# A planned kernel of attention, experts and a gated MLP: later planned landings, attention's tiles dealt out anew, a new order

## The chip, the cores and the metric

The kernel runs on one core of a Trainium2 chip. The metric is the device time of one execution in microseconds, the median of several runs. A profile is one further execution, taken by the hardware profiler. The engines of the core are TensorE (PE in the rows), VectorE (DVE), ScalarE (ACT), GpSimd (POOL) and SyncE (SP), which only issues transfers here. Each has a list of instructions of its own, which it works through in order.

## The reference

Three layers follow each other. The first is causal attention with a memory read beside it, over 4 batches, 8 heads, 576 positions and 64 columns:

```
scores = scale * q @ k.T ; causal ; a = softmax(scores) ; local = a @ v
q_p = where(q > 0, q, exp(q) - 1) + 1
mem_out = (q_p @ M_prev) / (q_p @ z_prev + 1e-6)
x = g * mem_out + (1 - g) * local          # g = sigmoid(beta)
```

The second sends each of the 2304 rows of x (512 wide) to one of 8 experts:

```
logits = x @ w_gate + modality_bias[modality_id] ; e_idx = argmax(logits)
out[rows of e] = gate_w * (relu(x @ w1[e]) @ w2[e])      # 512 -> 1024 -> 512
```

The third is a gated MLP over all rows, with weights of 512 x 1536, 512 x 1536 and 1536 x 512:

```
(silu(x @ w_gate) * (x @ w_val)) @ w_out
```

Everything is float32. The kernel gets that precision from fast products: an operand is split into a high and a low part, and three products (high x high, high x low, low x high) take the place of one.

## The kernel before, in words

The work runs in three phases that touch at their ends. **Attention** takes the 16 pairs of heads (4 in each batch) one after another, up to about 257 us of the profiled execution. For a pair, `pair(n)` turns k and q by TensorE into operands (L345, L351, and L362, L363 for the last 64 positions; they use the accumulator bank `prep`), splits them into high and low parts in a tile `HL`, makes the scores (L402 and L417, banks `ps`), masks them and takes the row maximum on VectorE (L410, L420, from `ps` into a tile `SS`), exponentiates on ScalarE (L422, `SS` into `PF`), turns the probabilities by TensorE (L432 into the banks `tp`, L441 into `mm`), copies them (L437, L438, into `pt`) and multiplies by v (L456 into the bank `LN`; L445 for the last 64 positions, into the bank `mm`). The memory products L377 read `mb` and `qp` and go into `mm` as well, and VectorE reads them in L380 to L384, and the result of L445 in L477. After each batch `route` computes the gate (L491, L497), using the modality ids `mi`, which VectorE casts once in L550. Near the end of attention, one expert is begun early: TensorE counts (L556), a register is read on SP, `rows()` reads three lists of 100 row numbers into `it` (L646), TensorE turns them (L647), GpSimd gathers the rows by them into `xr` (L652), and TensorE turns these (L654).

**The experts** follow, up to about 499 us: for blocks of 300 rows, `rows()` as before, then h products (L682 to L684) and y products (L670 to L672), with weights loaded in pieces of 512 KB into `raw` and split by `split`. **The gated MLP** is the rest: the products L787 to L789 (gate and value, into banks `gv`) and L805 to L807 (output, banks `po`). Its weights are converted by `split64` from 512 KB pieces of raw words: ScalarE L631, VectorE L633 to L636, ScalarE L637 (the high part) and GpSimd L638 (the low part). The last weights, in a place called `wC`, are still being converted while the products of this phase run.

The order is made by a planner, `Sched.run`, when the kernel is built. Each instruction or small group is a task with an engine, a duration as assumed, tasks that it needs, tiles that it takes from a pool and gives back, and a priority; in attention the table `PRM['off']` adds to the priority of each kind of task. The planner takes, over and over, the engine that can start first, and on it the task of best priority among those within the slack. For a transfer it assumes a landing:

```
s.way=max(s.way,t['end']+w)+t['dd']; t['lat']=s.way+w+200-t['end']+t['late']
```

So `late` is a time by which a transfer is assumed to land later. It is no wait on the chip; it sets where the planner puts the tasks that need the data. The order that results on each engine is fixed, and on the chip an instruction waits by semaphores for what it needs.

Of the kernel before, what the change touches and what calls it, by code (L numbers as in the profile page):

```python
# [10 lines left out]
F32 = mybir.dt.float32  # L11
F32R = mybir.dt.float32r
# [6 lines left out]
PSUM = bass.MemoryType.PSUM  # L19
# [8 lines left out]
def ac(n): return 60+.83*n  # L28
def po(n): return 150+2.1*n


PRM={'US': 1807, 'slack': 69, 'ps': (3, 2, 1, 1, 1), 'dcopy': (0,), 'off':{
# [10 lines left out]
NW=24; NC=4  # L43
# [8 lines left out]
class Sched:  # L52
# [18 lines left out]
    def add(s,eng,dur,fn,deps=(),acq=(),use=(),prio=0.0,lat=None,name='',ph=None):  # L71
# [5 lines left out]
        s.todo.append(t); return t  # L77
    def dma(s,fn,deps=(),acq=(),use=(),prio=0.0,nbytes=0,eng='SP',name='',ph=None,few=False,late=0.):
        t=s.add(eng,(650 if few else 500) if eng=='SP' else 1265,fn,deps,acq,use,prio,lat=1500+nbytes/360.,name=name,ph=ph)
        t['late']=late; t['dd']=max(30.,nbytes/360.); return t  # L80
    def ready(s,t):
# [95 lines left out]
class Net:  # L177
# [303 lines left out]
    warm=PRM.get("warm",(8,2,3))  # L481
# [132 lines left out]
    def split(s,src,prio,ph,lo_eng,deps=(),name=''):  # L614
        nc=s.nc; sc=s.sc; raw,hi,lo=sc.tok('raw'),sc.tok('w'),sc.tok('w')
        def f(): x=src(); nc.sync.dma_start(out=raw.tile.rearrange("p (k f) -> p k f",k=x.shape[1]),in_=x)
        d=sc.dma(f,deps=deps,acq=[raw],prio=prio,nbytes=524288,name='dw'+name,ph=ph,late=4000. if ph==2 else 2000. if ph==1 else 0.)
        a=sc.add('ACT',ac(1024)+37,lambda: nc.scalar.activation(out=hi.tile,in_=raw.tile,func=AF.Copy),deps=[d],acq=[hi],use=[raw],prio=prio,name='wh'+name,ph=ph)
        e=nc.gpsimd if lo_eng=='POOL' else nc.vector
        b=sc.add(lo_eng,po(1024) if lo_eng=='POOL' else dv(1024),lambda: e.tensor_tensor(lo.tile,raw.tile,hi.tile.bitcast(F32),op=ALU.subtract),deps=[a],acq=[lo],use=[raw,hi],prio=prio,name='wl'+name,ph=ph)  # L620
        return hi,lo,[a,b]

    def split64(s,src,prio,ph,name=''):
        nc=s.nc; sc=s.sc; hi,lo=sc.tok('w'),sc.tok('w'); dd=[]
        for h in range(2):
            raw,c=sc.tok('raw'),sc.tok('c'); sl=slice(512*h,512*h+512); p=prio+h
            def f(h=h,raw=raw): x=src(h); nc.sync.dma_start(out=raw.tile.bitcast(I32).rearrange("p (k f) -> p k f",k=x.shape[1]),in_=x)
            d=sc.dma(f,acq=[raw],prio=p,nbytes=524288,name='dw'+name,ph=ph,late=3000.)
            Hw=lambda raw=raw: raw.tile.bitcast(I32).rearrange("p (n w) -> p n w",w=2)[:,:,1]
# [14 lines left out]
    def rows(s,row,deps,prio,ph,ps,name='',nb=None):  # L644
        nc=s.nc; sc=s.sc; n=s.W//3; it,ii,xh,xl=sc.tok('it'),sc.tok('ii'),sc.tok('xh'),sc.tok('xl'); tp0=sc.tok(ps)
        d=sc.dma(lambda: s.after('ids',nc.sync.dma_start(out=it.tile,in_=s.idsE[bass.ds(row(),s.W),:].rearrange("(a c) o -> a (c o)",a=3))),deps=deps[0],acq=[it],prio=prio,name='id'+name,ph=ph,late=1000.)  # L646
        a=sc.add('PE',10,lambda: nc.tensor.transpose(tp0.tile[0:n,0:3],it.tile,s.ident[0:3,0:3]),deps=[d],acq=[tp0],use=[it],prio=prio+.1,name='it'+name,ph=ph)  # L647
        a=sc.add('DVE',75,lambda: nc.vector.tensor_copy(ii.tile[0:n],tp0.tile[0:n,0:3]),deps=[a],acq=[ii],use=[tp0],prio=prio+.2,name='ic'+name,ph=ph)
        dd=[]
        for j in range(3):  # L650
            xr=sc.tok('xr'); tp=sc.tok(ps); cs=slice(n*j,n*j+n)
            g=sc.dma(lambda j=j,xr=xr: nc.gpsimd.indirect_dma_start(out=xr.tile[0:n],out_offset=None,in_=s.xg if nb is None else s.xg[0:1+nb*s.S],in_offset=bass.IndirectOffsetOnAxis(ap=ii.tile[0:n,j:j+1],axis=0)),eng='POOL',deps=[a]+deps[1],acq=[xr],use=[ii],prio=prio+.3,nbytes=204800,name='gx'+name,ph=ph,late=2000.)  # L652
            def f(tp=tp,xr=xr):
# [192 lines left out]
def kernel(ctx0: ExitStack, tc: tile.TileContext, *aps: bass.AP):  # L846
# [4 lines left out]
    with ExitStack() as c0, tc.manual_schedule():  # L851
# [13 lines left out]
        for i,(k,k2) in enumerate((('xh','yh'),('xl','yl'))):  # L865
            v=[t.rearrange("p k c -> p (k c)")[:,0:4*W].rearrange("p (k c) -> p k c",k=4) for t in xx[i::2]]
            sc.pool(k,v); sc.pool(k2,[]); sc.give[k]={id(a):[(k2,t)] for a,t in zip(v,xx[i::2])}
        def some(p):
            s.tiles(p,'xr',2,[128,512]); s.tiles(p,'xtr',2,[128,4,128])
            sc.pools['raw']=sc.pools['raw'][:2]+[[p.tile([128,1024],F32,name="raw2"),0]]  # L870
# [5 lines left out]
        with ExitStack() as c1:  # L876
            pa=P(c1,"pa"); some(pa)
            for n,k,sh,dt in (('qn0',1,[128,4,256],F32),('kn0',1,[128,4,256],F32),('vn0',1,[128,5,256],F32),('qn1',1,[128,4,256],F32),('kn1',1,[128,4,256],F32),('vn1',1,[128,5,256],F32),('k4',2,[128,128],F32),
                          ('r2',1,[128,640],F32),('qp',1,[128,640],F32),('dn',2,[128,19],F32),('sm',2,[128,10],F32),('SS',2,[128,576],F32),('PF',3,[128,576],F32),('pt0',2,[128,2,256],F32),('pt2',2,[128,4,256],F32),('pt4',2,[128,640],F32),
                          ('oT',1,[128,512],F32),('t1',1,[128,4,2,64],F32),('t2',1,[128,4,2,64],F32),('t4',1,[128,128],F32)): s.tiles(pa,n,k,sh,dt)  # L880
            sc.pools['HL']+=[[pa.tile([128,2,1216],F32R,name=f"HL{i}"),0] for i in (1,2)]
            pp=P(c1,"pp",space=PSUM)
            for k,c in zip(('ps','tp','prep','LN','mm'),PRM['ps']): s.tiles(pp,k,c,[128,512])
            s.consts(pc,pa)
            s.plan1(); s.plan2(); s.plan3()
            sc.slack=PRM['slack']; sc.run(1); sc.slack=100
# [3 lines left out]
        with ExitStack() as c2:  # L890
            p2=P(c2,"p2"); some(p2); pp=P(c2,"pp2",space=PSUM)
            s.tiles(p2,'hh',3,[128,W],F32R); s.tiles(p2,'hl',3,[128,W],F32R)
# [46 lines left out]
```

## Time and profile before

| | |
|---|---|
| runs | 961.85, 962.27, 967.39 us |
| median | 962.27 us |
| profiled execution, its own time | 970.94 us |
| its span in the trace | 969.2 us |
| mean granted TensorE clock | 0.98 of full speed |
| TensorE busy | 929.1 us, 96% of the span |
| VectorE, ScalarE, GpSimd busy | 494.4, 392.1, 178.2 us |

The span is the time from the first to the last recorded instruction; 1.7 us lie around it. The profiled execution took 8.7 us longer than the median. All times inside the kernel, below and in the prediction, come from this one execution.

### The profile page before, as it was taken

To read this page: it belongs to the slowest core of one execution; us is meant where nothing else is said; L and a number is where in the kernel's file an instruction comes from. 1 tells how busy PE (TensorE), PEld (TensorE's weight loads), DVE (VectorE), ACT (ScalarE), POOL (GpSimd) and SP (SyncE) were. 2 spreads that over 40 slices of the span, in tenths; PEclk is the share of its full clock that TensorE was granted. 3 is DMA by queue.
4 is the path that set the end of the run, shared out by engine and by line. 5 is a ranking of instruction groups with operands and counts; after the bars stand their busy time and mean duration, and the time that the engine had idled before them with its cause. 6 is when DMAs were issued, how large, how long until landed. Compare 5 with 4: busy or idle time off the path is not lost. (4 is left out here: it accounts for less than half of the span.)

```text
span 969.2 us, 16634 instructions
## 1 busy us (share of the span) xinstructions
PE 929.1 (96%) x6389; PEld 846.4 (87%) x6389; DVE 494.4 (51%) x1382; ACT 392.1 (40%) x902; POOL 178.2 (18%) x199
## 2 busy tenths in 40 slices
PE   8899999997999999989989989999999999999996
PEld 7687786875798999989989989999999999999995
DVE  7787887896741538832556763223223223223221
ACT  6687888886633335412433332112112112112111
POOL 3112103122635423411221321001001001001001
PEclk9899999998999999999999999999999999999998
DMA  7444534214346634541222421001001000000000
GB/s 150 98 92 53 100 81 93 57 17 138 112 61 174 181 112 148 159 147 51 71 74 96 141 65 66 1 1 66 1 1 66 1 1 33 1 1 33 1 1 33
DMA packets 93426, 67.28 MB, mean 69 GB/s; under 512 B 67515, under 2 KB 78925, under 8 KB 93342
## 3 DMA queue, kind: packets, MB, share of 16 engines
q1 hardware_dynamic: 88797, 56.37, 23.2%
q0 software_dynamic: 4544, 9.79, 3.2%
q8 instruction: 52, 0.85, 0.4%
q14 instruction: 33, 0.26, 0.1%
HBM read 51.65 MB, written 14.49 MB: 68 GB/s over the span
## 5 line engine op out<-in xcount | busy, mean ns | idle before, releaser
L796 DVE SCALAR_TENSOR_TENSOR X<-X,gv 128x384 f32<-128x384 f32 x72 | 39.9, 554 | 188.7 <-ACT X L795 188.7
L787 PE MATMUL gv<-xx,wB 128*128 128x384 f32 x384 | 130.9, 341 | 2.0 <-PEq L822 2.0
L788 PE MATMUL gv<-xx,wB 128*128 128x384 f32 x384 | 130.7, 340 | 0.0
L789 PE MATMUL gv<-xx,wB 128*128 128x384 f32 x384 | 130.6, 340 | 0.0
L795 ACT ACTIVATE X<-gv 128x384 f32<-128x384 f32 x72 | 35.3, 491 | 199.4 <-PE gv L789 186.2
L422 ACT ACTIVATE PF<-SS,sm 128x256 f32<-128x256 f32 (+1 forms) x144 | 87.1, 607 | 12.2 <-DVE sm L410 8.8
L606 POOL DMA_INDIRECT out_dram<-X,ii x18 | 17.5, 971 | 360.5 <-ACT X L814 357.9
L787 PEld LDWEIGHTS gv<-xx,wB 128*128 128x128 f32 x384 | 72.5, 189 | 4.3 <-issue 2.2
L788 PEld LDWEIGHTS gv<-xx,wB 128*128 128x128 f32 x384 | 72.6, 189 | 1.9
L789 PEld LDWEIGHTS gv<-xx,wB 128*128 128x128 f32 x384 | 72.7, 189 | 0.0
L797 DVE TENSOR_TENSOR X<-X,gv 128x384 f32<-128x384 f32 x72 | 39.9, 554 | 63.5 <-PE gv L789 63.2
L687 DVE SCALAR_TENSOR_TENSOR hl<-h,hh 128x300 fp32r<-128x300 f32 x64 | 29.9, 467 | 77.8 <-ACT hh L686 75.5
L410 DVE CUSTOM_DVE_ANT_0 SS<-ps,mk 128x256 f32<-128x256 f32 (+2 forms) x128 | 64.5, 517 | 5.2 <-PE prep L351 1.9
L432 PE MATMUL tp<-ident,PF 128*128 128x128 f32 x384 | 63.6, 287 | 1.3 <-ACT pt L438 1.2
L438 ACT ACTIVATE pt<-tp 128x512 f32<-128x512 f32 (+2 forms) x112 | 54.6, 501 | 21.6 <-PE tp L432 16.5
L686 ACT ACTIVATE hh<-h 128x300 fp32r<-128x300 f32 x64 | 26.7, 418 | 87.1 <-PE h L684 84.3
L682 PE MATMUL h<-xx,wB 128*128 128x300 f32 x192 | 59.1, 308 | 0.0
L684 PE MATMUL h<-xx,wB 128*128 128x300 f32 x192 | 58.3, 303 | 0.0
L683 PE MATMUL h<-xx,wB 128*128 128x300 f32 x192 | 58.1, 303 | 0.0
L807 PE MATMUL po<-wB,al 128*128 128x512 f32 x144 | 56.7, 394 | 0.0
L432 PEld LDWEIGHTS tp<-ident,PF 128*128 128x128 f32 x384 | 43.6, 144 | 11.6 <-issue 3.6
L638 POOL TENSOR_TENSOR wB<-X,wB 128x512 fp32r<-128x512 f32 x24 | 33.5, 1400 | 90.0 <-ACT wB L637 52.4
(287 smaller groups left out, 2368.5 us busy)
## 6 DMA issues: line engine op xcount, KB each, us to landing
raw<-in_moe_w_dram SPq DMA_DIRECT2D x16, 512.0 KB
raw<-in_moe_w_gate_dram SPq DMA_DIRECT2D x12, 512.0 KB
raw<-in_moe_w_val_dram SPq DMA_DIRECT2D x12, 512.0 KB
raw<-in_moe_w_out_dram SPq DMA_DIRECT2D x12, 512.0 KB
yT<-X SPq DMA_DIRECT2D x8, 600.0 KB
X<-yT SPq DMA_DIRECT2D x6, 768.0 KB
kn<-in_k_dram SPq DMA_DIRECT2D x32, 128.0 KB
qn<-in_q_dram SPq DMA_DIRECT2D x32, 128.0 KB
```

The lines of the kernel that those rows point to most:

```text
L410: def f(Sp=Sp,SS=SS,i=i,N=N,c=c,so=so): nc.vector.tensor_tensor_reduce(out=SS.tile[:,0:N],in0=Sp.tile[:,so:so+N],in1=s.mk[:,512-128*i:512- ...
L422: def f(SS=SS,PF=PF,N=N,c=c): nc.scalar.activation(out=PF.tile[:,0:N],in_=SS.tile[:,0:N],func=AF.Exp,scale=-1.0,bias=sm.tile[:,c:c+1],accu ...
L432: for j in range(m+1): nc.tensor.transpose(tp.tile[:,128*j:128*j+128],PF.tile[:,128*j:128*j+128],s.ident)
L438: else: cps.append(add('ACT',ac(W),lambda pc=pc,tv=tv: nc.scalar.activation(out=pc(),in_=tv(),func=AF.Copy),deps=[Tt],prio=pu+2*US,name=f' ...
L682: nc.tensor.matmul(o,H,xh.tile[:,k],start=(k==0),stop=False)
L683: nc.tensor.matmul(o,H,xl.tile[:,k],start=False,stop=False)
L684: nc.tensor.matmul(o,Lo,xh.tile[:,k],start=False,stop=(k==3))
L787: nc.tensor.matmul(o,H,yh.tile[:,k],start=(k==0),stop=False)
L788: nc.tensor.matmul(o,H,yl.tile[:,k],start=False,stop=False)
L789: nc.tensor.matmul(o,Lo,yh.tile[:,k],start=False,stop=(k==3))
L796: a=sc.add('DVE',dv(TN),lambda th=th,g=g: nc.vector.scalar_tensor_tensor(out=th.tile,in0=th.tile,scalar=1.0,in1=g.tile[:,0:TN],op0=ALU.add ...
L807: nc.tensor.matmul(o,lv()[:,c],H,start=False,stop=(f==NF-1))
```

## The change

It has three parts. The first: the planner assumes later landings. A transfer of attention with a positive priority gets 2500 ns where it had none; the weight pieces of the experts (`split`) get 4000 in any phase that is named, where it was 2000 or 4000; those of the MLP (`split64`) 3000 or 500, where it was 3000; the row numbers (L646) 4500 or 3500, where it was 1000; the gathers (L652) 3500, where it was 2000. The second: in attention there are four tiles `xr` (before: two), three `SS` (two), four `PF` (three) and two `HL` (three). The accumulator banks stay as they were (three `ps`, two `tp`, one each of `prep`, `LN` and `mm`). The third: all numbers of the table `PRM['off']` are new. Cut to its core:

```
-    'AV,5':-0.98, 'AV,7':4.14, 'AV,8':-6, 'S,0':5.55, 'S,2':4.03, 'S,3':3.22, 'S,8':4.36, 'T,0':-4.86, 'T,1':-3.23, 'T,2':-1.64, 'T,3':-3.04,
+    'AV,5':6, 'AV,7':-5.67, 'AV,8':-4.47, 'S,0':4.42, 'S,2':5.94, 'S,3':4.15, 'S,8':3.99, 'T,0':-5.64, 'T,1':-5.59, 'T,2':-3.75, 'T,3':-5.07,
...
-    def dma(s,fn,deps=(),acq=(),use=(),prio=0.0,nbytes=0,eng='SP',name='',ph=None,few=False,late=0.):
+    def dma(s,fn,deps=(),acq=(),use=(),prio=0.0,nbytes=0,eng='SP',name='',ph=None,few=False,late=None):
-        t['late']=late; t['dd']=max(30.,nbytes/360.); return t
+        t['late']=(2500. if ph is None and s.ph==1 and prio>0 else 0.) if late is None else late; t['dd']=max(30.,nbytes/360.); return t
...
-        d=sc.dma(f,deps=deps,acq=[raw],prio=prio,nbytes=524288,name='dw'+name,ph=ph,late=4000. if ph==2 else 2000. if ph==1 else 0.)
+        d=sc.dma(f,deps=deps,acq=[raw],prio=prio,nbytes=524288,name='dw'+name,ph=ph,late=4000. if ph else 0.)
...
-            d=sc.dma(f,acq=[raw],prio=p,nbytes=524288,name='dw'+name,ph=ph,late=3000.)
+            d=sc.dma(f,acq=[raw],prio=p,nbytes=524288,name='dw'+name,ph=ph,late=3000. if ph==2 else 500.)
...
(rows: the row numbers, late=1000. -> late=4500. if ph==1 else 3500.; the gathers, late=2000. -> late=3500.)
...
-            s.tiles(p,'xr',2,[128,512]); s.tiles(p,'xtr',2,[128,4,128])
+            s.tiles(p,'xr',n,[128,512]); s.tiles(p,'xtr',2,[128,4,128])
...
-            pa=P(c1,"pa"); some(pa)
+            pa=P(c1,"pa"); some(pa,4)
...
-('SS',2,[128,576],F32),('PF',3,[128,576],F32)
+('SS',3,[128,576],F32),('PF',4,[128,576],F32)
...
-            sc.pools['HL']+=[[pa.tile([128,2,1216],F32R,name=f"HL{i}"),0] for i in (1,2)]
+            sc.pools['HL']+=[[pa.tile([128,2,1216],F32R,name=f"HL{i}"),0] for i in (1,)]
...
-            p2=P(c2,"p2"); some(p2); pp=P(c2,"pp2",space=PSUM)
+            p2=P(c2,"p2"); some(p2,2); pp=P(c2,"pp2",space=PSUM)
```

TensorE has 5111 rows of instructions before and after. Three places show what moved on it.

On TensorE near the end of attention, where the first row numbers of the early expert are turned (L647; HL2 and HL1 are copies of the tile HL, it0 and it1 the row numbers). Before:

```order
L402 MATMUL ps1_138<-HL2_133 128x512
L402 MATMUL ps0_137<-HL2_133 128x512
L432 MATMUL tp1_141<-ident_145,PF2_121 128x128 x2
L377 MATMUL mm0_144<-mb1_152,qp0_112 128x130 x3
L647 MATMUL ps2_139<-ident_145,it0_75 100x3
L351 MATMUL prep0_142<-ident_145,qn10_106 128x128 x4
L647 MATMUL ps1_138<-ident_145,it1_76 100x3
```

After:

```order
L402 MATMUL ps2_142<-HL1_136 128x256
L402 MATMUL ps0_140<-HL1_136 128x256
L362 MATMUL prep0_145<-ident_148,k41_112 128x128
L363 MATMUL prep0_145<-ident_148,q4_1_153 128x128
L647 MATMUL ps1_141<-ident_148,it0_75 100x3
L432 MATMUL tp0_143<-ident_148,PF2_124 128x128 x4
L647 MATMUL ps1_141<-ident_148,it1_76 100x3
```

The first L647 was row 866 of TensorE's list and is row 891 now; the count at L556, on which the row numbers depend, is row 792 in both. Between the two stand twelve L402 of 256 columns, ten L432, six L417, four L456, four L351, two L377, one L362 and one L363 more than before.

On TensorE between pairs 5 and 6 (L377 is the first memory product of pair 6, into the bank mm0; the last product of pair 5, L445, goes into the same bank and stands just ahead of six L402 of 384 columns in both lists, the last two of which are the first rows here). Before:

```order
L402 MATMUL ps1_138<-HL_72 128x384
L402 MATMUL ps0_137<-HL_72 128x384
L432 MATMUL tp1_141<-ident_145,PF1_120 128x128
L432 MATMUL tp0_140<-ident_145,PF0_119 128x128 x2
L351 MATMUL prep0_142<-ident_145,qn10_106 128x128 x4
L377 MATMUL mm0_144<-mb1_152,qp0_112 128x130 x3
```

After:

```order
L402 MATMUL ps1_141<-HL_72 128x384
L402 MATMUL ps0_140<-HL_72 128x384
L377 MATMUL mm0_147<-mb1_155,qp0_114 128x130 x3
L467 MATMUL tp0_143<-ident_148,oT0_132 128x128 x4
L432 MATMUL tp1_144<-ident_148,PF0_122 128x128 x2
L351 MATMUL prep0_145<-ident_148,qn10_108 128x128 x4
```

Three L432 and four L351 stood between the last L402 and L377, and nothing does now. The distance from L445 to L377 is shorter than before at the ends of pairs 1, 5, 11 and 14.

On TensorE in the expert phase, at the transposes of gathered rows (L654, from the tiles xr0 and xr1) of the sixth block. Before:

```order
L672 MATMUL y30_3379<-hl1_3370,wB14_3345 128x300
L654 MATMUL xp1_3375<-ident_145,xr0_3358 128x100 x4
L654 MATMUL xp0_3374<-ident_145,xr1_3359 128x100 x4
L682 MATMUL h1_3373<-xx2_82,wB16_3347 128x300
L683 MATMUL h1_3373<-xx3_83,wB16_3347 128x300
L684 MATMUL h1_3373<-xx2_82,wB17_3348 128x300
```

After:

```order
L682 MATMUL h1_3376<-xx2_82,wB16_3350 128x300
L683 MATMUL h1_3376<-xx3_83,wB16_3350 128x300
L684 MATMUL h1_3376<-xx2_82,wB17_3351 128x300
L654 MATMUL xp1_3378<-ident_148,xr0_3361 128x100 x4
L654 MATMUL xp0_3377<-ident_148,xr1_3362 128x100 x4
L670 MATMUL y00_3379<-hh2_3371,wB18_3352 128x300
```

The two L654 stood right behind the y products, ahead of the h products of the next step, and stand behind twelve of them now.

Two moves lie on other engines. On SP the eight loads of `mi` are the 33rd to 40th transfer of its list, where they were the 39th to 46th, and VectorE's cast of them (L550) stands ahead of two L410 of 512 columns that it stood behind. In the MLP the conversions of the last weights stand earlier on ScalarE (L631, L637) and on VectorE (L633 to L636), by about one of the steps that L795 marks; GpSimd's and SP's lists in that phase are the same.

## Rows read from the trace of the kernel before

**Rows 1.** The page: busy time by engine, and the granted clock of TensorE in 40 slices.

```profile
PE 929.1 (96%) x6389; PEld 846.4 (87%) x6389; DVE 494.4 (51%) x1382; ACT 392.1 (40%) x902; POOL 178.2 (18%) x199
...
PEclk9899999998999999999999999999999999999998
```

**Rows 2.** Waits of TensorE by releaser: us in total, times, longest us.

```profile
PE ps L647 <- DMA it<-idsE: 3.7, 1, 3.7
...
PE gv L787 <- ACT wC L637: 1.9, 1, 1.9
```

**Rows 3.** Windows: length, busy us (x instructions) of each engine, PEclk, DMA share, GB/s.

```profile
25.00:50.00 25.00, 22.03 (x192) 17.57 (x187) 18.61 (x70) 16.93 (x47) 4.14 (x5) 0.86 0.51 104
425.00:450.00 25.00, 22.71 (x157) 22.33 (x157) 5.56 (x12) 4.88 (x11) 2.00 (x2) 0.93 0.13 41
550.00:575.00 25.00, 22.28 (x107) 20.14 (x106) 16.63 (x28) 7.57 (x14) 5.14 (x4) 0.93 0.31 90
```

**Rows 4.** Timeline of VectorE, 27 to 33 us: start, duration, instruction, [idle before, releaser].

```profile
27.53 0.69 DVE L410 CUSTOM_DVE_ANT_0 SS<-ps,mk 128x512 f32<-128x512 f32 x1
...
31.19 0.18 DVE L550 CAST mf<-mi 128x20 f32<-128x20 int32 x1 [2.97 <-DMA mi<-in_moe_modality_id_dram]
```

**Rows 5.** Timeline of SP's queue, 23 to 31 us.

```profile
23.82 0.39 SPq L256 DMA_DIRECT2D mi<-in_moe_modality_id_dram  x1
...
27.81 0.52 SPq L257 DMA_DIRECT2D mi<-in_moe_modality_id_dram  x1
```

**Rows 6.** Timeline of SP's queue, 205 to 232 us.

```profile
216.13 0.74 SPq L616 DMA_DIRECT2D raw<-in_moe_w_dram  x1
220.41 0.79 SPq L646 DMA_DIRECT2D it<-idsE  x2
```

**Rows 7.** Timeline of TensorE, three places from 204 to 229 us.

```profile
204.66 0.17 PE L556 MATMUL ps<-cum,ones 128*1 128x8 bf16 x1
...
209.14 0.94 PE L377 MATMUL mm<-mb,qp 128*128 128x130 f32 x6 [0.66 <-DVE X L477]
...
228.09 0.21 PE L647 MATMUL ps<-ident,it 3*100 3x3 f32 x1 [3.68 <-DMA it<-idsE]
```

**Rows 8.** Timeline of TensorE, 242 to 246.8 us, the last pair.

```profile
242.03 0.79 PE L402 MATMUL ps<-HL 64*128 64x384 f32 x6
242.76 0.80 PE L445 MATMUL mm<-vn,pt 128*64 128x64 f32 x20
243.49 0.55 PE L432 MATMUL tp<-ident,PF 128*128 128x128 f32 x3
243.96 1.06 PE L402 MATMUL ps<-HL 64*128 64x512 f32 x6
...
245.23 0.83 PE L377 MATMUL mm<-mb,qp 128*128 128x130 f32 x6
245.82 1.03 PE L417 MATMUL ps<-HL 128*128 128x288 f32 x6
246.70 0.33 PE L432 MATMUL tp<-ident,PF 128*128 128x128 f32 x1
```

**Rows 9.** Windows at the end of attention, columns as in rows 3.

```profile
228.09:240.00 11.91, 10.30 (x69) 8.33 (x70) 9.46 (x32) 7.14 (x18) 4.44 (x3) 0.77 0.31 89
240.00:257.70 17.70, 15.45 (x154) 12.60 (x155) 15.43 (x44) 13.34 (x32) 13.63 (x9) 0.99 0.47 137
```

**Rows 10.** Timeline of TensorE in the expert phase, two places.

```profile
427.68 0.64 PE L654 MATMUL xp<-ident,xr 100*128 100x100 f32 x4 [2.29 <-DMA xr<-xg,ii]
...
490.87 0.30 PE L682 MATMUL h<-xx,wB 128*128 128x300 f32 x1
491.01 0.30 PE L683 MATMUL h<-xx,wB 128*128 128x300 f32 x1
```

**Rows 11.** Timeline of ScalarE, 509 to 521 us, two gate steps of the MLP.

```profile
514.29 0.49 ACT L795 ACTIVATE X<-gv 128x384 f32<-128x384 f32 x1 [3.41 <-PE gv L789]
...
520.58 0.49 ACT L795 ACTIVATE X<-gv 128x384 f32<-128x384 f32 x1
```

More of the change, by code (lines that the diff above doesn't have):

```diff
@@ L645, in rows @@
         nc=s.nc; sc=s.sc; n=s.W//3; it,ii,xh,xl=sc.tok('it'),sc.tok('ii'),sc.tok('xh'),sc.tok('xl'); tp0=sc.tok(ps)
-        d=sc.dma(lambda: s.after('ids',nc.sync.dma_start(out=it.tile,in_=s.idsE[bass.ds(row(),s.W),:].rearrange("(a c) o -> a (c o)",a=3))),deps=deps[0],acq=[it],prio=prio,name='id'+name,ph=ph,late=1000.)
+        d=sc.dma(lambda: s.after('ids',nc.sync.dma_start(out=it.tile,in_=s.idsE[bass.ds(row(),s.W),:].rearrange("(a c) o -> a (c o)",a=3))),deps=deps[0],acq=[it],prio=prio,name='id'+name,ph=ph,late=4500. if ph==1 else 3500.)
         a=sc.add('PE',10,lambda: nc.tensor.transpose(tp0.tile[0:n,0:3],it.tile,s.ident[0:3,0:3]),deps=[d],acq=[tp0],use=[it],prio=prio+.1,name='it'+name,ph=ph)
@@ L651, in rows @@
             xr=sc.tok('xr'); tp=sc.tok(ps); cs=slice(n*j,n*j+n)
-            g=sc.dma(lambda j=j,xr=xr: nc.gpsimd.indirect_dma_start(out=xr.tile[0:n],out_offset=None,in_=s.xg if nb is None else s.xg[0:1+nb*s.S],in_offset=bass.IndirectOffsetOnAxis(ap=ii.tile[0:n,j:j+1],axis=0)),eng='POOL',deps=[a]+deps[1],acq=[xr],use=[ii],prio=prio+.3,nbytes=204800,name='gx'+name,ph=ph,late=2000.)
+            g=sc.dma(lambda j=j,xr=xr: nc.gpsimd.indirect_dma_start(out=xr.tile[0:n],out_offset=None,in_=s.xg if nb is None else s.xg[0:1+nb*s.S],in_offset=bass.IndirectOffsetOnAxis(ap=ii.tile[0:n,j:j+1],axis=0)),eng='POOL',deps=[a]+deps[1],acq=[xr],use=[ii],prio=prio+.3,nbytes=204800,name='gx'+name,ph=ph,late=3500.)
             def f(tp=tp,xr=xr):
@@ L867, with some @@
             sc.pool(k,v); sc.pool(k2,[]); sc.give[k]={id(a):[(k2,t)] for a,t in zip(v,xx[i::2])}
-        def some(p):
-            s.tiles(p,'xr',2,[128,512]); s.tiles(p,'xtr',2,[128,4,128])
+        def some(p,n):
+            s.tiles(p,'xr',n,[128,512]); s.tiles(p,'xtr',2,[128,4,128])
             sc.pools['raw']=sc.pools['raw'][:2]+[[p.tile([128,1024],F32,name="raw2"),0]]
@@ L876 @@
         with ExitStack() as c1:
-            pa=P(c1,"pa"); some(pa)
+            pa=P(c1,"pa"); some(pa,4)
             for n,k,sh,dt in (('qn0',1,[128,4,256],F32),('kn0',1,[128,4,256],F32),('vn0',1,[128,5,256],F32),('qn1',1,[128,4,256],F32),('kn1',1,[128,4,256],F32),('vn1',1,[128,5,256],F32),('k4',2,[128,128],F32),
-                          ('r2',1,[128,640],F32),('qp',1,[128,640],F32),('dn',2,[128,19],F32),('sm',2,[128,10],F32),('SS',2,[128,576],F32),('PF',3,[128,576],F32),('pt0',2,[128,2,256],F32),('pt2',2,[128,4,256],F32),('pt4',2,[128,640],F32),
+                          ('r2',1,[128,640],F32),('qp',1,[128,640],F32),('dn',2,[128,19],F32),('sm',2,[128,10],F32),('SS',3,[128,576],F32),('PF',4,[128,576],F32),('pt0',2,[128,2,256],F32),('pt2',2,[128,4,256],F32),('pt4',2,[128,640],F32),
                           ('oT',1,[128,512],F32),('t1',1,[128,4,2,64],F32),('t2',1,[128,4,2,64],F32),('t4',1,[128,128],F32)): s.tiles(pa,n,k,sh,dt)
-            sc.pools['HL']+=[[pa.tile([128,2,1216],F32R,name=f"HL{i}"),0] for i in (1,2)]
+            sc.pools['HL']+=[[pa.tile([128,2,1216],F32R,name=f"HL{i}"),0] for i in (1,)]
             pp=P(c1,"pp",space=PSUM)
```

18 rows, old and new, of the table PRM are left out of this document.

## The prediction, made before the changed kernel was timed

> **What bounds the kernel now.** I read the page's busy line first: TensorE is busy for 929.1 us, VectorE for 494.4, ScalarE for 392.1 [rows 1]. TensorE runs one fixed list of instructions, so the time is its work plus its waits plus what its clock loses. The clock line of [rows 1] gives 0.9 or more in 37 of 40 slices and 0.8 in three (the second, the tenth, the last), so full speed is lost in short places. Next I read the list of waits on TensorE by releaser: it names no large sum, only single waits of a few us [rows 2]. The third view, windows with the granted clock, shows that such a wait costs more than itself [rows 3]. In 25 to 50 us TensorE is idle for 2.97 us, and the clock is 0.86, which loses another 3.5 us of full-speed work (25 x 0.14); in 425 to 450 it is 2.29 us and 0.93 (1.75 us); in 550 to 575 it is 2.72 us and 0.93 (1.75 us). So the question for this change is which of these waits the new order closes, and which it opens.
>
> The profiled execution took 970.94 us, the median is 962.27, 8.7 us less. I make the sum in the profiled execution and carry it to the median unchanged; that the 8.7 us may lie in the very waits that I count is a rival below.
>
> **What the change adds and removes.** No instruction of TensorE is added or removed, so its work stays. The late figures are numbers in the planner and no commands; they act through the order alone. The extra buffers (two for gathered rows, one for scores, one for probabilities) let GpSimd, VectorE and ScalarE run ahead where they waited for a tile. In attention no long wait of TensorE is put down to such a tile, so I price them at nothing (the cover is that VectorE is busy for half the span, ScalarE for less; without it, a fraction of a us in a pair). The third copy of the split operands goes: a pair then needs the copy of the pair two before it, which has been read out by then; nothing.
>
> **The modality ids, early (gain 2.3 us).** VectorE's cast of the ids waited 2.97 us for their loads until 31.19 [rows 4], and TensorE's second memory product of that pair waited behind it. The eight loads were issued from 23.82 to 27.81, one per 0.57 us [rows 5]. In the new order of SP's queue they stand six places earlier, some 3.7 us with what lay between. But the cast also stands earlier on VectorE, ahead of two score passes of 0.69 us [rows 4], 1.4 us. So 2.97 - 3.7 + 1.4 leaves 0.7 of the wait, and 2.3 us go. Ends: nothing, if the loads land no earlier for being issued earlier, and 2.3 + 3.5 = 5.8, if all that the clock loses there [rows 3] comes back. I take 2.3, the end nearer to the row, since some of the wait is left for the clock to fall after.
>
> **The row numbers of the early expert (gain 6.4 us).** This is the largest single wait. The read of 1.2 KB was issued at 220.41, the last of three weight loads of 512 KB ahead of it at 216.13 [rows 6], and TensorE waited 3.68 us for it until 228.09 [rows 7]. In the new order TensorE has more to do between L556 (204.66) and L647: twelve L402 of 256 columns more, ten L432, six L417, two L377 and ten others. By [rows 8] six L402 of 384 columns take 0.73 us (242.03 to 242.76), so twelve of 256 some 1.0; three L432 0.47 (243.49 to 243.96), so ten 1.6; six L417 0.88 (245.82 to 246.70); two of six L377 0.2 (245.23 to 245.82). That is 3.7 us, and the others come on top, so the wait is filled. Behind it the clock was 0.77 from 228.09 to 240.0 [rows 9], a loss of 11.91 x 0.23 = 2.7 us. Together 6.4. Ends: 3.7, if the clock falls all the same, after another wait, and 10.3, if the idle time of the two windows of [rows 9] (11.91 - 10.30 and 17.70 - 15.45, together 3.9 us) goes as well, since the gathers now have a buffer each.
>
> What [rows 6, 7] show is a read of 1.2 KB that took 7.7 us behind 1.5 MB of weights. [...]
>
> **The sixth gather of the expert phase (gain 3.4 us).** TensorE waited 2.29 us for gathered rows until 427.68 [rows 10]. The transposes now stand twelve h products later; two of these start 0.14 us apart (490.87, 491.01), so 1.7 us are filled and 0.6 is left. With the clock's 1.75 us [rows 3] that is 3.4. Ends: 1.7 with the clock as it was, and 4.0.
>
> **The converted weights of the last phase (gain 4.5 us).** TensorE waited 1.9 us at L787 for ScalarE's copy of a weight [rows 2], and the window around it has 2.72 us of idle time in all [rows 3]. On ScalarE and VectorE the conversions now stand about one gate step earlier; two such steps lie 6.29 us apart (514.29, 520.58) [rows 11]. That is more than the wait, so I count all of it and the clock's 1.75 us. Ends: nothing, if the conversions then wait for their raw weights, and 4.5.
>
> **New waits on the memory bank (loss 3.0 us).** One accumulator bank (mm) takes the last product of a pair, L445, and then the next pair's L377, which must wait until VectorE has read it (L477). At 209.14 L377 waited 0.66 us for that [rows 7]. Where there was no wait, 1.74 us of other work stood between (243.49 to 245.23) [rows 8]. In the new order the distance shrinks in four pairs; between pairs 5 and 6 it is six L402 of 384 columns, 0.73 us. So two places lack about 1.0 us each and two others about 0.5: 3.0. Ends: nothing, if VectorE reads at once, and 7, if it reads 0.66 us and more behind its place, as at 209.14, and a clock fall follows once.
>
> [...]
>
> **Sum.** -2.3 - 6.4 - 3.4 - 4.5 + 3.0 = -13.6 us. From the median: 962.3 - 13.6 = **948.7**. With all gains at their upper ends and no new wait, -24.6 us: 937.7. With all at their lower ends, 0 - 3.7 - 1.7 - 0 + 7 = +1.6: 963.9.
>
> **Rivals.**
> (a) The waits belong to the profiled execution. It was 8.7 us over the median; if that lies in the waits counted, 13.6 - 8.7 = 4.9 us are left: **957.4**. For it: reads that land a few us late can vary from one execution to the next. Against it: the waits have fixed places in the list, and half of the sum is behind an order that repeats.
> (b) The change moves the plan and not the chip. The loads land when the queue ahead of them is through, so the ids and the gathered rows come no earlier, and the work that stands ahead of L647 now waits itself, for VectorE, so that nothing is filled. Left are the weights' 4.5 and the new waits' 3.0: **960.8**. For it: VectorE is what released the wait at 209.14. Against it: that row is 0.66 us, not 3.7.
> (c) Slower: the single bank. If the wait between L445 and L377 comes to some 2.7 us and the clock falls behind it, as in the window from 550 [rows 3], a place costs 2.72 + 1.75 = 4.5 us. Against a sum of -13.6 it takes six such places to lose over 9.6: 962.3 - 13.6 + 6 x 4.5 = **975.7**. For it: the distance shrinks in four pairs, to 0.73 us in one. Against it: at 209.14 the wait was 0.66, and four pairs are not six.
>
> **How the numbers follow.** Chances: the forecast 0.57, (a) 0.20, (b) 0.16, (c) 0.07. One per cent, 9.6 us, is about what a measurement of this kernel can tell from no change; the bounds are 952.6 and 971.9. The forecast lies under 952.6 in 0.53 of its 0.57, and of (a) a part does (0.04): faster 0.57. Slower is (c), 0.07, and the rest, 0.36, is the same. The range leaves out (c) and the outermost ends: from 939, near all gains at once, to 962, which takes in (a) and (b).
>
> **What would show it.** In the profile after: no wait of L647 on the row numbers near 228 us and a clock of 0.9 or more from there to 240; the end of attention about 6 to 9 us earlier; no wait of L787 on wC; the wait on xr near 414 under 1 us; and in the list of waits L377 on VectorE's X with 2 to 4 us in all. Wrong would be: L647 still waiting 3 us, so that the moved work did not run ahead, or a list in which L377, L362 and L402 wait over 10 us for VectorE, so that the order costs what it saves.

## The result, and the profile after

The changed kernel takes 955.18 us (median of 4 runs, 952.51 to 956.18) beside 964.43 for the kernel before on the same chip (4 runs): a ratio of 0.9899, 95% interval 0.9856 to 0.9941. Run again in a second set of runs (e5 below) it took 951.21 us beside 965.36, a ratio of 0.9849 (0.9792 to 0.9907). So it is faster by 1.0 to 1.5 per cent, 9 to 14 us. The prediction was 948.7, a gain of 13.6.

The profiled execution took 954.26 us, 16.7 less than that of before. The busy and clock lines of its page, against [rows 1]:

```profile
PE 921.6 (97%) x6389; PEld 841.0 (88%) x6389; DVE 491.4 (52%) x1382; ACT 388.7 (41%) x902; POOL 177.3 (19%) x199
...
PEclk9999999999999999999999999999999999999999
```

TensorE's work is the same, its clock is 0.9 or more in every slice. The list of waits on TensorE is another one, against [rows 2] (releaser: us in total, times, longest):

```profile
PE y L672 <- DVE hl L687: 2.8, 3, 1.9
PE mm L441 <- DVE t L390: 2.8, 1, 2.8
PE gv L787 <- PEq L822: 2.0, 1, 2.0
PE mm L445 <- ACT pt L438: 1.8, 1, 1.8
PE h L683 <- DVE xx L658: 1.7, 2, 1.5
```

L647's wait for the row numbers and L787's for its weight are gone, and waits for VectorE stand at the top. (The 2.0 us of L787 behind TensorE's own sequencer, PEq, stand in the list of before as well.) The windows of [rows 3] (columns: length, busy us of each engine, PEclk, DMA share, GB/s), with two that the prediction did not count:

```profile
25.00:50.00 25.00, 24.86 (x233) 19.76 (x235) 22.67 (x92) 20.86 (x61) 3.98 (x5) 1.00 0.68 146
225.00:250.00 25.00, 19.49 (x178) 16.50 (x176) 17.55 (x42) 14.91 (x34) 15.26 (x10) 0.86 0.35 106
300.00:325.00 25.00, 22.42 (x154) 21.75 (x153) 13.53 (x21) 9.66 (x18) 13.49 (x9) 0.93 0.56 177
425.00:450.00 25.00, 25.00 (x187) 24.81 (x186) 5.89 (x13) 5.06 (x12) 3.01 (x3) 1.00 0.16 48
550.00:575.00 25.00, 25.00 (x133) 23.41 (x132) 13.90 (x23) 8.63 (x16) 5.86 (x9) 1.00 0.20 66
```

The three windows that the prediction named have their full clock now, and less idle time. Idle time and a low clock stand in two other places: at the end of attention, where TensorE is idle for 5.5 us, and in the first blocks of the experts. So the sign "a clock of 0.9 or more" behind L647 did not come: it is 0.86 from 225 to 250, and no higher from 228 to 240, where before had 0.77.

To see where the time went, I read three stages from each profile: attention up to the first h product (the first L682), the experts up to the first L787, and the MLP from there to the end of the span. Attention took 258.45 us before and takes 247.69; the experts 241.11 and 240.13; the MLP 469.60 and 464.66. These are differences of -10.8, -1.0 and -4.9.

The timeline of TensorE after, in five places, shows the stages' edges and the waits at the top of the list:

```profile
220.92 0.21 PE L647 MATMUL ps<-ident,it 3*100 3x3 f32 x1
...
242.07 0.30 PE L441 MATMUL mm<-ident,PF 128*128 128x128 f32 x1 [2.79 <-DVE t L390]
...
247.69 0.41 PE L682 MATMUL h<-xx,w 128*128 128x300 f32 x1 [0.90 <-DVE xx L658]
...
316.54 0.40 PE L672 MATMUL y<-hl,w 128*128 128x300 f32 x1 [1.92 <-DVE hl L687]
...
487.82 0.42 PE L787 MATMUL gv<-xx,wB 128*128 128x384 f32 x1 [1.96 <-PEq L822]
```

### The profile page after: what moved, and what is told of

Read it like the earlier page. It is cut to its first block, busy times and chain, and to the rows that moved or that the text cites. A ratio compares the mean times of both kernels' runs of the same rounds, so it can differ in the third digit from the quotient of the medians.

```text
span 952.5 us, 16582 instructions
## 1 busy us (share of the span) xinstructions
PE 921.6 (97%) x6389; PEld 841.0 (88%) x6389; DVE 491.4 (52%) x1382; ACT 388.7 (41%) x902; POOL 177.3 (19%) x199
## 5 line engine op out<-in xcount | busy, mean ns | idle before, releaser
L787 PE MATMUL gv<-xx,wB 128*128 128x384 f32 x384 | 130.7, 340 | 2.0 <-PEq L822 2.0
L795 ACT ACTIVATE X<-gv 128x384 f32<-128x384 f32 x72 | 35.4, 491 | 190.0 <-PE gv L789 176.9
L787 PEld LDWEIGHTS gv<-xx,wB 128*128 128x128 f32 x384 | 72.5, 189 | 4.3 <-issue 2.2
L687 DVE SCALAR_TENSOR_TENSOR hl<-h,hh 128x300 fp32r<-128x300 f32 x64 | 30.0, 468 | 81.9 <-ACT hh L686 81.6
L410 DVE CUSTOM_DVE_ANT_0 SS<-ps,mk 128x256 f32<-128x256 f32 (+2 forms) x128 | 64.8, 518 | 7.9 <-PE ps L402 5.7
L432 PE MATMUL tp<-ident,PF 128*128 128x128 f32 x384 | 61.7, 281 | 1.7 <-ACT pt L438 1.3
L438 ACT ACTIVATE pt<-tp 128x512 f32<-128x512 f32 (+2 forms) x112 | 55.0, 506 | 16.1 <-PE tp L432 13.9
L683 PE MATMUL h<-xx,wB 128*128 128x300 f32 x192 | 57.6, 300 | 1.5 <-DVE xx L658 1.5
L682 PE MATMUL h<-xx,wB 128*128 128x300 f32 x192 | 57.9, 302 | 0.0
L684 PE MATMUL h<-xx,wB 128*128 128x300 f32 x192 | 57.6, 300 | 0.0
L432 PEld LDWEIGHTS tp<-ident,PF 128*128 128x128 f32 x384 | 43.5, 141 | 8.8 <-ACT pt L438 3.6
L670 PE MATMUL y<-hh,wB 128*128 128x300 f32 x160 | 49.1, 307 | 1.0 <-DVE X L693 1.0
```

What stands on the lines that cost most here:

```text
L410: def f(Sp=Sp,SS=SS,i=i,N=N,c=c,so=so): nc.vector.tensor_tensor_reduce(out=SS.tile[:,0:N],in0=Sp.tile[:,so:so+N],in1=s.mk[:,512-128*i:512- ...
L432: for j in range(m+1): nc.tensor.transpose(tp.tile[:,128*j:128*j+128],PF.tile[:,128*j:128*j+128],s.ident)
L438: else: cps.append(add('ACT',ac(W),lambda pc=pc,tv=tv: nc.scalar.activation(out=pc(),in_=tv(),func=AF.Copy),deps=[Tt],prio=pu+2*US,name=f' ...
L670: nc.tensor.matmul(o,H,hh.tile,start=(fb==0),stop=False)
L682: nc.tensor.matmul(o,H,xh.tile[:,k],start=(k==0),stop=False)
L683: nc.tensor.matmul(o,H,xl.tile[:,k],start=False,stop=False)
```

## The experiments

Each kernel below was profiled once and timed in rounds beside the kernel before; e1 to e4 shared one chip and one set of runs of before, e5 to e8 another, e9 to e12 the first again. The planner's later landings act by phase, so the order of one phase can be had with the order of another, or nearly so.

**e1: before, with the MLP's weight landings of the change.**

```
-  (split64) late=3000.
+  (split64) late=3000. if ph==2 else 500.
```

> The kernel before with one figure changed: the landing of the gated MLP's weight pieces is planned 500 ns late, not 3000. The orders of attention and of the experts are those of before, that of the MLP is that of the change. If the conversions' place is what took the wait at L787 away (theory A): the MLP stage, from the first L787 to the end of the span, takes 464.7 us as in the changed kernel and not 469.6, no wait of L787 on wC, and the time is about 4.9 us under before. If the wait belonged to the one profiled execution of before (theory B): the time is within 2 us of before. The other two stages show whether before's waits repeat: by A the row numbers' wait at L647 is again 3 to 4 us and attention ends near 258 us; by B one of the two is over 2 us shorter.

It took 958.38 us beside 962.12, ratio 0.9946 (0.9917 to 0.9975). The MLP stage took 464.63 us. The window of e1's profile in which before had the wait at L787:

```profile
550.00:575.00 25.00, 25.00 (x133) 23.38 (x132) 17.92 (x29) 9.52 (x17) 5.20 (x5) 1.00 0.14 45
```

No idle time and the full clock: theory A. The wait at L647 was there again, 5.0 us, and attention ended at 258.82.

**e2: the change, with the MLP's landings of before** (the same line, the other way).

> The changed kernel with that one figure put back to 3000 ns. Attention and experts in the order of the change, the MLP in the order of before. Theory A: the wait at L787 is back with 1.5 to 3 us and a low clock behind it, the MLP stage takes 469.6 us and the time is about 4.9 us over the changed kernel's. Theory B: no such wait, and the time is within 2 us of the changed kernel's. Attention ends near 247.7 us, with the 2.8 us wait of L441, if the changed order repeats.

It took 953.17 us beside 962.12, ratio 0.9898 (0.9864 to 0.9932). The wait of 1.9 us at L787 was back and the MLP stage took 469.67 us, as A has it. In all, the stage took 464.5 to 464.7 us in the seven profiles with the new order and 469.3 to 470.7 in the seven with the old one. Attention ended at 242.15 us, 5.5 earlier than in the first profile of the changed kernel, whose attention has the same order; so one profile tells a length of attention to some 5 us only.

**e3: before, with the experts' landings of the change.**

```
-  (row numbers) late=1000.
+  (row numbers) late=1000. if ph==1 else 3500.
-  (gathers) late=2000.
+  (gathers) late=2000. if ph==1 else 3500.
```

> The kernel before with the landings of the row numbers and gathers of the expert phase planned late as in the change (3500 ns each, not 1000 and 2000). Attention and MLP in the order of before, the experts nearly in that of the change. Theory A: the wait of 2.3 us on the sixth gather is gone, but waits for gathered rows elsewhere in the phase take its place as in the changed profile, and the expert stage takes about 240 us (before 241.1), so the time is 0 to 2 us under before. Theory B (the new waits of the expert phase in the changed profile were chance): the stage takes 236 to 238 us, 3 to 5 us under before. The MLP stage of before repeats: 469.6 us with the wait at L787 by A, 465 by B.

It took 967.82 us beside 962.12, ratio 1.0072 (1.0041 to 1.0103): slower by 4 to 10 us, which neither theory had. The waits of the changed kernel were there, as it had them: L672 on VectorE's hl 2.9 us, L683 on xx 1.7. Its profile does not show the loss: that execution took 959.88 us, 7.9 under the median, and its expert stage 239.59, as theory A has it, beside 241.11 in before and 238.63 in e1.

**e4: the change, with the experts' landings of before.**

> The changed kernel with those landings of the expert phase put back (1000 and 2000 ns). Attention and MLP in the order of the change, the experts nearly in that of before. Theory A: the wait on the sixth gather is back (1.5 to 3 us), the waits of the changed kernel inside the experts' blocks (VectorE's hl and xx, 1.9 and 1.5 us) are gone, and the expert stage takes about 241 us, so the time is 0 to 2 us over the changed kernel's. Theory B: the stage takes 238 us or less and this kernel is faster than the changed one.

It took 944.16 us beside 962.12, ratio 0.9830 (0.9789 to 0.9871): the fastest of all kernels here. The expert stage took 236.64 us, against 240.13, 241.86 and 238.45 in the three profiles with the changed order there and the changed attention. The wait on the sixth gather was back (1.44 us) and the two waits on VectorE were gone. Theory B was the nearer.

On one chip e1 to e4 form a square. With the MLP in its new order, the new attention and the old experts (e4) stand 14.2 us under the old attention and the old experts (e1). With the MLP in its old order, the new attention and the new experts (e2) stand 14.7 us under the old attention and the new experts (e3). So the attention of the change is worth some 14 us, give or take 5 by the intervals, and its MLP some 4 (e1). The medians put a cost of 4 to 6 us on its expert order (e3 over before by 5.7; e2 over e4 by 9.0, of which 4.9 is the MLP), but only the first of the two is clear of the spread of the runs, and the lengths of the stage do not bear it out: the ten profiles with the old expert order, or nearly it, have 235.0 to 243.8 us, 239.8 in the mean, and the four with the new one 238.5 to 241.9, 240.0 in the mean.

**e5: the changed kernel again.**

> The changed kernel once more, beside the next three kernels on one chip. If the three stages add up as runs e1 to e4 say (attention some 14.4 us less, the experts some 5 more, the MLP some 4 less: theory A), it takes 13 to 14 us less than before, a ratio of 0.986. If the first comparison's 0.990 is the size of it (theory B), 9 to 10 us less.

951.21 us beside 965.36, ratio 0.9849 (0.9792 to 0.9907), 14.2 us: nearer to theory A, though the interval takes in 9 us too. The waits repeat: L441 2.8 us, L672 1.9 us.

**e6: the change, with all landings of row numbers and gathers of before.** Same two lines as e3, both phases back to 1000 and 2000.

> The changed kernel with the landings of the row numbers and gathers put back in attention and in the experts (1000 and 2000 ns). In attention TensorE then has 16.8 us of work by its own spacing between L556 and the first L647, where the change has 20.1 and before had 15.4. Theory A (the work that was moved ahead of L647 filled the wait): L647 waits 3 to 5 us again, and from L556 to the first h product 50 to 54 us pass, where the changed kernel has 45 to 50; beside e4, which has the same landings in the experts, it is 4 to 7 us slower. Theory B (the wait went for another reason, as a shorter queue ahead of the read): no wait over 1 us, 45 to 50 us, as fast as e4.

It took 951.72 us beside 965.36, ratio 0.9866 (0.9807 to 0.9926). The timeline of its TensorE at the end of attention:

```profile
196.65 0.17 PE L556 MATMUL ps<-cum,ones 128*1 128x8 bf16 x1
...
217.30 0.18 PE L647 MATMUL ps<-ident,it 3*100 3x3 f32 x1 [1.59 <-DMA it<-idsE]
```

L647 waited 1.59 us, not 3 to 5, and the time from L556 to the first h product was 44.7 us, the shortest in any profile. So 1.6 us of wait at L647 do not make the end of attention long; a wait of 3 to 5 us, on which theory A rests, did not occur. The read itself was quicker here. On SP, in before:

```profile
214.28 0.47 SPq L544 DMA_DIRECT2D xg<-X  x1
...
215.44 0.48 SPq L544 DMA_DIRECT2D xg<-X  x1
...
220.41 0.79 SPq L646 DMA_DIRECT2D it<-idsE  x2
```

and in e6:

```profile
208.46 1.60 SPq L616 DMA_DIRECT2D raw<-in_moe_w_dram  x3
212.43 0.79 SPq L646 DMA_DIRECT2D it<-idsE  x2
213.33 1.46 SPq L544 DMA_DIRECT2D xg<-X  x3
```

TensorE had the row numbers 4.9 us after the issue in e6 and 4.5 in e12 below, against 7.7 in before, 7.5 in e1, 7.6 in e3 and 6.9 in e10. So part of the wait went for another reason than the moved work, as theory B has it. Two stores of x (L544) stood between the three weight loads ahead of the read in before, and none stands between them in e6; that this is the reason no run shows by itself.

In the profiles e6 loses most against e4 in the experts (241.22 us, with a wait of 3.6 us for a later read of row numbers). With the old expert order it is no faster than the changed kernel of e5.

**e7: before, with the later landings in attention alone.**

```
+  (default) 2500. in attention for a positive priority
-  (split) 2000. in attention        +  4000.
-  (row numbers) 1000. in attention  +  4500.
-  (gathers) 2000. in attention      +  3500.
```

> The kernel before with the later landings in attention alone; its table and its tiles as before. It has 19.0 us of work between L556 and L647. Theory A: the wait at L647 is 0 to 2 us, 47 to 50 us pass from L556 to the first h product where before has 53 to 56, and the time is 5 to 7 us under before; the rest of attention keeps the waits of before. Theory B: within 2 us of before.

It took 965.42 us beside 965.36, ratio 1.0004 (0.9977 to 1.0031): nothing. Its list of waits on TensorE:

```profile
PE ps L654 <- DMA xr<-xg,ii: 4.2, 3, 1.8
PE tp L467 <- DVE pt L437: 3.7, 1, 3.7
```

The wait at L647 was gone, as the work moved ahead of it would have it, and two others stood there: for gathered rows, of which before, e1 and e3 had 0.5 to 1.9 us in attention, and for VectorE. The second comes from one instruction of VectorE (usually 0.22 us), which ran beside two subtractions of GpSimd; the last section comes back to this:

```profile
224.01 4.69 DVE L367 TENSOR_SCALAR r<-r 128x128 f32<-128x128 f32 x1
...
223.95 4.66 POOL L620 TENSOR_TENSOR w<-raw,w 128x1024 fp32r<-128x1024 f32 x2
```

So e7 shows that the later landings alone bring nothing. What the filled wait would be worth without the new ones it does not show. From L556 to the first h product 56.0 us passed, against 53.8, 55.8 and 52.8 in the profiles with before's own order.

**e8: before, with the new table alone.** One edit: the numbers of the table.

> The kernel before with the new table of priorities alone; landings and tiles as before. It has 16.0 us of work between L556 and L647, so by theory A L647 waits 3 to 5 us and from L556 to the first h product 52 to 56 us pass; ahead of that the ids are loaded early as in the change, so pair 1 takes 11.8 us where before took 14.8 in two of three profiles, and all in all the kernel is 2 to 6 us under before. By theory B (the table was made for the new tiles, and without them it brings nothing) it is no faster than before, or slower by the waits for scores' and probabilities' tiles.

It took 961.39 us beside 965.36, ratio 0.9966 (0.9931 to 1.0000), 4 us by the medians, at the edge of its interval. Pair 1, from its first L362 to that of the next pair, took 13.84 us, not 11.8. From L556 to the first h product 53.0 us: the table alone does not shorten the end of attention.

**e9: e4, with two gather tiles in attention.**

```
-  some(pa,4)
+  some(pa,2)
```

> Kernel e4 with two tiles for gathered rows in attention, as before, where it has four; the order differs from e4 in a few places of the last pair only. Theory A (it is the two more gather tiles that shorten the end of attention): the six gathers go in pairs again, each pair after the transposes of the one ahead; from the first L654 to the first h product 18 to 20 us pass, as in all profiles with two tiles, where e4 has 13.9; the kernel is 3 to 5 us slower than e4. Theory B (the table's order shortens it): 14 to 16 us, and within 1.5 us of e4.

It took 960.49 us beside 966.05, ratio 0.9950 (0.9921 to 0.9978), where e4 has 0.9830 on the same chip: 1.2 per cent, some 12 us, for two tiles. From the first L654 to the first h product 23.0 us passed (e4: 13.9). GpSimd's timeline in e9:

```profile
234.18 1.01 POOL L652 DMA_INDIRECT xr<-xg,ii  x1 [0.30 <-PE ps L654]
235.21 2.38 POOL L620 TENSOR_TENSOR w<-raw,w 128x1024 fp32r<-128x1024 f32 x1
237.53 4.65 POOL L620 TENSOR_TENSOR HL<-raw,w 128x1024 fp32r<-128x1024 f32 x2
247.43 1.01 POOL L652 DMA_INDIRECT xr<-xg,ii  x1 [5.24 <-PE ps L654]
```

and in e4:

```profile
221.06 0.99 POOL L652 DMA_INDIRECT xr<-xg,ii  x1 [0.31 <-issue]
222.35 1.01 POOL L652 DMA_INDIRECT xr<-xg,ii  x1 [0.30 <-issue]
227.20 1.01 POOL L652 DMA_INDIRECT xr<-xg,ii  x1 [0.18 <-issue]
228.51 1.00 POOL L652 DMA_INDIRECT xr<-xg,ii  x1 [0.31 <-issue]
```

With two tiles the last gather but one waited until TensorE had turned the pair ahead of it and was issued at 247.43; TensorE then stood for it (L654, 4.4 us). With four it was issued at 227.20, and no L654 of attention waited. Theory A, and by more than it said.

The gathers are one half of it. The tiles also move GpSimd's subtractions: three (L620) stand in a row in e9 from 235.21, a VectorE instruction took 7.07 us beside them, and TensorE's L441 behind it waited 5.80 (rows of e9):

```profile
235.14 7.07 DVE L382 TENSOR_TENSOR dn<-dn,gate 128x4 f32<-128x4 f32 x1
...
243.17 0.45 PE L441 MATMUL mm<-ident,PF 128*128 128x128 f32 x1 [5.80 <-DVE t L390]
...
251.90 0.93 PE L654 MATMUL ps<-ident,xr 100*128 100x100 f32 x4 [4.42 <-DMA xr<-xg,ii]
```

The window from L647 to the first h product, e4 first, then e9 (columns as above):

```profile
216.76:239.60 22.84, 18.36 (x182) 14.42 (x181) 20.95 (x60) 17.18 (x43) 16.44 (x12) 1.00 0.35 108
219.46:255.08 35.62, 23.10 (x182) 18.42 (x181) 25.30 (x60) 17.61 (x43) 18.01 (x12) 0.79 0.29 94
```

TensorE is idle for 8.0 us more, and its clock is 0.79 in place of 1.00. Of the waits that e4 has not, 4.6 us are for gathered rows, 2.9 at L441 and 1.7 at an L402 are for VectorE.

**e10: before, with a third gather tile.** One edit: three tiles in attention, not two.

> The kernel before with a third tile for gathered rows in attention and nothing else; four do not fit beside its other tiles. The orders differ from before at the end of attention and a little in the experts. Theory A: three gathers go at once, 15 to 17 us from the first L654 to the first h product (before 18.4), and 2 to 4 us under before. Theory B: 18 to 20 us, and within 1.5 us of before.

It took 968.64 us beside 966.05, ratio 1.0050 (1.0009 to 1.0091): not faster. From the first L654 to the first h product 20.3 us passed, though three gathers went one after another. So with before's table and landings a tile more brings nothing; it has to come with an order that uses it. Where the loss lies the profile does not show: its execution took 962.76 us, 5.9 under the median, with an L647 wait of 2.4 us in attention and one of 3.8 in the experts, whose stage took 240.58.

**e11: before, with the new tiles alone.**

> The kernel before with the new tiles alone (four for gathered rows, three for scores, four for probabilities, two for operands); table and landings as before. Theory A: 14 to 16 us from the first L654 to the first h product, and 4 to 7 us under before. Theory B (the tiles help only in the order of the new table): no faster than before; the waits of earlier pairs, L362 and L377 on VectorE, are as large or larger.

It took 978.91 us beside 966.05, ratio 1.0154 (1.0106 to 1.0202), 13 us slower. Its list of waits on TensorE (the first stands in the experts):

```profile
PE xp L647 <- DMA it<-idsE: 5.5, 1, 5.5
PE tp L432 <- ACT pt L438: 5.5, 3, 4.6
PE tp L467 <- DVE pt L437: 4.5, 1, 4.5
PE mm L377 <- DVE X L477: 2.7, 1, 2.7
```

Theory B. With the old table and the new tiles the planner makes an order in which TensorE waits for ScalarE and VectorE in several pairs; pair 13 took 24.2 us, against 19.2 to 19.7 in the three profiles of before's attention (before, e1 and e3). The new tiles take one copy of HL away as well as adding others; no run separates the two.

**e12: new tiles, new table, and the MLP's landings; nothing else late.**

> New tiles, new table and the 500 ns of the MLP's weights; all other landings as before, so neither attention nor the experts are planned late. Theory A (later landings gain nothing in attention, as e7 says, and cost time in the experts, as e3 and e4 say): as fast as e4, 17 to 20 us under before. Theory B (they gain in attention in the new order): L647 waits 3 to 5 us, and the kernel is 4 to 7 us slower than e4.

It took 958.16 us beside 966.05, ratio 0.9919 (0.9891 to 0.9946), against 0.9830 for e4, which has the later landings in attention as well. So the landings that bring nothing in before's order (e7) are worth something here, as theory B says, but not at L647, which waited 1.6 us: TensorE waited 3.8 us at an L654 for VectorE, the experts took 243.76 us with an L647 wait of 5.4 there, and attention 249.20 where e4 took 239.60. The end of attention is long here although four tiles are there and the last gather was issued at 229.84: from L556 to the first h product 51.7 us (e4: 45.1), from the first L654 21.5 (13.9). Rows of VectorE, GpSimd and TensorE:

```profile
234.07 5.03 DVE L382 TENSOR_TENSOR dn<-dn,gate 128x6 f32<-128x6 f32 x1
...
232.09 4.69 POOL L620 TENSOR_TENSOR w<-raw,w 128x1024 fp32r<-128x1024 f32 x2
236.73 2.34 POOL L620 TENSOR_TENSOR HL<-raw,w 128x1024 fp32r<-128x1024 f32 x1
...
239.77 0.56 PE L654 MATMUL ps<-ident,xr 100*128 100x100 f32 x4 [3.84 <-DVE sm L410]
```

Again three subtractions stand in a row, and an instruction of VectorE takes 5.03 us beside them.

## Why the prediction was right, and where it was not

**The sum was right, its terms were not all.** 13.6 us were forecast; 9.3 and 14.2 were measured in two comparisons. By the medians of e1 to e4 the three stages give -14, +5 and -4, where the forecast's terms give -5.7 (ids, row numbers and bank), -3.4 and -4.5. Attention brought more than was forecast and the experts brought no gain; that the sum came out is in good part luck.

**The converted weights: right in mechanism and size.** Forecast 4.5, measured 4.9 in the first pair of profiles, 4.6 to 6.2 in any pair, and 3.7 by the medians of e1. It is the one term that stands alone: the wait at L787 for wC (1.9 us in before and e2, none in after and e1) and the clock's loss around it (0.93 from 550 to 575 in before, 1.00 in after and e1) go with the conversions' place.

**The modality ids: right in direction.** VectorE's cast started at 28.39 without a wait:

```profile
28.39 0.17 DVE L550 CAST mf<-mi 128x20 f32<-128x20 int32 x1
```

against 31.19 in [rows 4]. Pair 1 took 11.80 to 11.84 us in all profiles of the changed order with its landings. It took 14.83, 15.19 and 10.85 in the three with before's, and 11.47 in e10, which differs from before only further on. So this wait is long in some executions of before and short in others, and what rival (a) said of it holds: the gain is 1.3 us by the means, not 2.3.

**The row numbers of the early expert: the wait went, but that was not the gain.** The step that failed is "The extra buffers ... I price them at nothing", with its cover. L647 waits no more in the changed kernel, and from L556 to the first h product 45.1 to 49.7 us pass in the four profiles of e2, e4, e5 and the first, where before, e1 and e3 took 52.8 to 55.8: 7.0 us by the means, about the 6.4 forecast. The wait went for two reasons, of which the prediction had one: TensorE had more to do ahead of L647, and the read came sooner, by some 2.7 us in the means of the runs in which TensorE waited for it (e6; the changed kernel has the same order of transfers there). But e7 fills the wait in before's order and gains nothing, and e6 lets 1.6 us of it stand and loses nothing there.

What the runs showed in its place is the gather tiles, in an order that uses them: e9 takes two of the four away, and the 13.9 us behind the first L654 become 23.0. In before, the six gathers went in pairs, issued from 230.6, 240.8 and 249.6, each pair after TensorE had turned rows of the one ahead; the prediction saw this only as a reason for an upper end. The tiles alone are not the cause. In e9 some 4.6 us are the gathers' own and 4.6 are waits for VectorE beside subtractions that moved with the tiles, and e12 has four tiles, early gathers and a long end all the same. The cover was wrong too: VectorE is busy for half the span, but for 15.43 of the last 17.70 us of attention [rows 9]. Order, tiles and landings need each other: tiles alone lose (e11), the table alone gains little (e8), the landings alone nothing (e7), and in e12 tiles and table without the landings give half of what e4 gives.

**The sixth gather: the wait went, the gain did not come.** The step is "The transposes now stand twelve h products later" and the 3.4 us put on it. The wait at that L654 went, as it said: the four profiles with the new expert order list none there, the ten others 1.4 to 2.5 us. It did not ask what the later transposes make late in the next blocks: L672 then waits 1.9 us for VectorE, L683 1.5, and the clock is 0.93 in the window from 300. All four profiles with this order have these waits; in the ten others L672 waits 0.7 us for hl at most and no wait of L683 is listed. The new order does close the experts' waits for row numbers (1.3 us at most, where the old one has up to 5.5). In before's attention it loses 4 to 10 us (e3). Beside the changed attention the medians of e2 and e4 say a loss of 4, which is within the spread, and e6 with the old order is no faster. So that the 3.4 us did not come is shown, and how large the loss is in the changed kernel stays open.

**The memory bank: right in size by luck, wrong in mechanism.** L377 waited 0.3 us in all for VectorE and not at all for L477; so the shorter distance from L445 cost next to nothing. But L441, which takes the same bank, waited 2.8 or 2.9 us for the memory product to be read (L390) in the four profiles of the change, e2, e4 and e5, and 5.8 in e9. The term said 3.0. This wait goes with the long L382 of VectorE beside GpSimd (4.77 us after, last section): in e6, where no instruction of VectorE is that long there, L441 does not wait.

**Rivals.** (c) did not come. (a) holds in part: attention with before's order took 249.0 to 258.8 us in three profiles, so the profiled execution of before was among the long ones. (b) has its outcome in e7, for the landings alone, but not its mechanism: the wait at L647 was filled there, and in the new order the read came sooner (e6: 4.9 us after its issue, before: 7.7).

What stays open: how much of attention's gain is due to the tiles for scores and probabilities, which no run took away by themselves; how much of the gather tiles' worth goes by way of GpSimd's subtractions, which moved with them; and why the length of attention differs by up to 10 us between executions of one order.

## What to carry to other kernels

A wait that is filled is no gain until the next thing behind it is known to be early: in e7 other waits took its place (4.2 and 3.7 us), and in e9 the tiles of the gathers, not the first wait, set the end. A change of tiles also moved the other work of the engine that fills them, GpSimd's subtractions, beside which one instruction of VectorE took 7.07 us in e9; so look at what runs beside it. Order, buffers and planned times were changed together here, and their effects did not add; of attention's three parts each alone brought 0.3 per cent at most, and one lost 1.5. Changes that act in separate phases can be told apart by crossing the phases, and one part left out then gave a kernel better than both: e4, 0.983 of before.

## What the runs showed of the hardware

The new waits on VectorE at the two places that the result named, and those in e7, e9 and e12, go with one thing in the rows: an instruction of VectorE that took far longer than usual. After, the timelines of VectorE

```profile
236.34 4.77 DVE L382 TENSOR_TENSOR dn<-dn,gate 128x4 f32<-128x4 f32 x1
...
312.24 3.14 DVE L634 TENSOR_SCALAR X<-X 128x512 int32<-128x512 int32 x1
```

and of GpSimd, in the same two places:

```profile
236.42 2.37 POOL L620 TENSOR_TENSOR w<-raw,w 128x1024 fp32r<-128x1024 f32 x1
238.73 2.35 POOL L620 TENSOR_TENSOR HL<-raw,w 128x1024 fp32r<-128x1024 f32 x1
...
312.69 2.41 POOL L620 TENSOR_TENSOR wB<-raw,wB 128x1024 fp32r<-128x1024 f32 x1
```

The L382 of 4 columns takes 0.16 us in the median of the profile after; here it ended at 241.11, when the two subtractions of GpSimd had ended (241.08), and in e9, where three of them stood there, it took 7.07 us and L441 waited 5.8. In the fourteen profiles every instruction of VectorE in attention and the experts that took over 0.5 us more than the median of its kind (line and shape) ran beside a TENSOR_TENSOR of GpSimd, 5 to 18 of them in each profile. The converse does not hold: none of the 792 instructions of L343, L410, L437, L658, L687 and L693 that ran beside one, all of which read an accumulator bank, took that much longer, while 12 of 31 of L382, which reads two SBUF tiles, did. In the experts the time above the median adds up to 13.0 to 14.1 us in the four profiles with the new order and to 3.9 to 6.6 in the ten others. The 4.77 us after lie beside two subtractions that followed each other at once (236.42 to 241.08), the 7.07 of e9 beside three (235.21 to 242.18). Why an instruction of 0.16 us takes that long beside them no run shows. No run here moved the subtractions to another engine, so what that would be worth is not shown.
